# Lists of tokens: weights and columns of each list matmul laid side by side, made by thirds, multiplied in bursts of 16

## The chip, the cores and the metric

The kernel runs on one core of a Trainium2 chip. The metric is the device time of one execution in microseconds; the profile shows one execution. PE is TensorE, DVE VectorE, ACT ScalarE, POOL GpSimd, SP the queue that issues most DMAs. PEld is the loading of a matmul's weights. [...]

## The reference, cut to what matters

```python
N, D, E, F = 24576, 256, 8, 1024          # after FFT over (3072, 256) of 8 batches and a bilinear layer
logits = x @ w_gate                        # [N, E]
cap = N // E                               # 3072
for idx in np.argsort(-logits.flatten()):  # best pairs first
    tok, e = idx // E, idx % E
    if assigned[tok] >= 0 or counts[e] >= cap: continue
    assigned[tok] = e; counts[e] += 1
for e in range(E):
    mask = assigned == e
    out[mask] = np.maximum(x[mask] @ w1[e], 0.0) @ w2[e]
```

First come the Fourier transform of `x` along the sequence and the features (real part) and the layer `((x@w1) * (x@w2) @ w3) @ w_out`. Then each token goes to one of eight experts by the greedy rule above, each expert takes exactly 3072 tokens, and each expert is two matrices with a ReLU between.

## The kernel before, in words

Stage A (to about 1440 us) computes transform and layer and leaves 24576 rows in DRAM (`xs_d`) and the logits `L` in SBUF, as 128 partitions by 192 tiles (NT = 192) for each of the eight experts. The last part of its products is put off (`putoff`, L1338) and serves as TensorE's work while the first list is made.

Stage B works in eight phases (`ph`). For each phase `route` (L1121) finds which expert fills next, by two searches of eight counting rounds each for the 3072nd best logit, and then makes the **list** of the 3072 tokens of that expert, 24 of them in each of 128 partitions (CT = 24). The list is used as the index of gathers from DRAM (`gather`, L1407).

How the list is made: every token has a position 0 to 3071, or none. `rb` holds for each token (partition p, tile j) the row r (position modulo 128) and the column c (position divided by 128, plus 1). The list's entry (r, c) is the number of the token, 128 j + p. It is a sum over j of outer products: for each of the 192 tiles one matmul `li += oR[:, r | j]^T @ oC[:, c | j]` (L1281), with 128x128 bf16 weights that hold 1 where the token of partition p in tile j has row r, and 48 columns: 24 with p and 24 with j, where its column is c. `oR` and `oC` are made by comparisons on DVE: `X8` holds r minus a for a = 0..7, `C4` c minus a for a = 0..3 (L1256), and one instruction compares `X8` with 8r' to give eight rows at once (L1270), or `C4` with 4c'+1 for four columns (L1261). ACT makes the plane with p (L1262), DVE multiplies the other one by j (L1276). The tile number j is the innermost index, so the 128 weights of one matmul stand H elements apart (H = 60 in the first part) and its 48 columns 192 elements apart. `oR` is made in parts of 60, 60, 56 and 16 tiles (`PARTS`, L1039) in two buffers, and after each part its matmuls are issued in one block.

The order of work in stage B is written out by the program itself. The loop at L1583 goes over phases, six groups (`g`) of 512 tokens, and eight blocks (`f`) of 128 hidden units, here called steps. A step issues `first` (L1446: six matmuls of 512 columns into `hp`, L220 to L222), and `flush`/`second` (L1477: twelve of 256 columns into `yp`, L1487) for the step two before (LAG = 2). In f = 4 and 6 `turned` (L1429) transposes a block of the next group (L1432); DVE finishes it with L1440, and the split of the hidden values with L1470. ACT's share is L1436 and L1466.

Between these the routes run as generators: `lists()` (L1525) is called four times in a step and takes the next pieces of the route as long as the planner's clocks permit. The clocks are sums of estimated costs: `use("pe", 0.655)` for half of a `first` or `second`, a `yield` of so many us for DVE work, `use("a", ...)` for ACT. A `yield -2` holds the route until PE's planned clock has passed the others; a `yield -1` ends the call. When group 5 of a phase begins, the list of the next phase is demanded:

```python
if g == G - 1 and f == 0 and ph + 1 < E:
    while len(done) < ph + 2:
        next(gens[0])
    st = weights(which[ph + 1])
```

What is left of that list is then issued at once, whatever the clocks say. Each engine works through its own instructions in the order of issue. In the first route (L1557) there are no expert products yet, and each `yield` pays for steps of `putoff`, one per STEP = 0.26.

Of the kernel before, what the change touches and what calls it, by code (L numbers as in the profile page):

```python
# [9 lines left out]
F32 = mybir.dt.float32  # L10
F32R = mybir.dt.float32r
BF = mybir.dt.bfloat16
I32 = mybir.dt.int32
U32 = mybir.dt.uint32
U16 = mybir.dt.uint16
AF = mybir.ActivationFunctionType
ALU = mybir.AluOpType
# [5 lines left out]
NT = N // 128  # L23
CAP = N // E
CT = CAP // 128
# [995 lines left out]
def stage_b(ctx, tc, I, out, k):  # L1021
    nc, vec, act, pool = k.nc, k.vec, k.act, k.pool
    Lw = k.L
    cp_ = ctx.enter_context(tc.tile_pool(name="rconst", bufs=1))
# [6 lines left out]
    tri, trij, jrow, rank, ones = (rc[n].bitcast(BF) for n in ("tri", "trij", "jrow", "rank", "ones"))  # L1031
    pcol, rank9, id8, srch = (rc[n] for n in ("pcol", "rank9", "id8", "srch"))
# [3 lines left out]
    sg4, thr1, neg3 = srch[:, 64:68], srch[:, 68:71], srch[:, 71:74]  # L1036
    ident = k.sc["ident"]
    CHAIN = 0.45
    PARTS = (60, 60, 56, 16)  # L1039
    rt = ctx.enter_context(tc.tile_pool(name="rt", bufs=2))  # L1040
    ex = ctx.enter_context(tc.tile_pool(name="ex", bufs=2))
    blk = cp_.tile([128, 128], F32R, name="blk")
# [6 lines left out]
    vec.memset(zero, 0.0)  # L1049
    ecs = cp_.tile([128, 1], F32, name="ecs")  # L1050
    vec.memset(ecs, float(E * (E + 1) // 2))
    alive = cp_.tile([128, NT], F32, name="alive")
    vec.memset(alive, 1.0)

# [9 lines left out]
    clock = {"pe": 0.0, "v": 0.0, "a": 0.0, "d": 0.0}  # L1064

    def use(engine, cost, after=0.0):
        clock[engine] = max(clock[engine], after) + cost
        return clock[engine]


    def whole(b):
        return [128, b, NT]
# [18 lines left out]
    def small(shape, name, dt=F32):  # L1091
        return rt.tile([128] + shape, dt, name=name)
# [28 lines left out]
    def route(ph, done):  # L1121
# [3 lines left out]
        if ph < E - 1:  # L1125

            v = rt.tile([128, NT], F32, name="v", bufs=1)
            vec.tensor_reduce(v, Lw.rearrange("p e j -> p j e"), axis=AX.X, op=ALU.max)
            yield 1.7
            oh = rt.tile([128, E, NT], BF, name="X8", bufs=1)  # L1130
            vec.tensor_tensor(oh, Lw, v[:, None, :].to_broadcast(whole(E)), op=ALU.is_equal)
            yield 1.7
            vec.tensor_tensor(oh, oh, rank, op=ALU.mult)
            yield 0.9
            m4 = rt.tile([128, 4, NT], BF, name="C4", bufs=1)
            vec.tensor_tensor(m4, oh[:, 0:4], oh[:, 4:8], op=ALU.max)
            vec.tensor_tensor(m4[:, 0:2], m4[:, 0:2], m4[:, 2:4], op=ALU.max)
            code = rt.tile([128, NT], BF, name="code", bufs=1)
# [9 lines left out]
            hl = rt.tile([128, 2, NT], U16, name="hlv", bufs=1)  # L1148
            vec.tensor_tensor(hl, ky.bitcast(U16).rearrange("p (j h) -> p h j", h=2), alive[:, None, :].to_broadcast(whole(2)), op=ALU.mult)
            yield 0.9  # L1150
            planes = rt.tile([128, 2, CT, NT], BF, name="oC", bufs=1).rearrange("p a c j -> p (a c j)").bitcast(U16)
            quart = rt.tile([128, 128 * PARTS[0]], BF, name="oR", bufs=2).bitcast(U16)
            quart = [quart[:, i * E * NT:(i + 1) * E * NT] for i in range(4)]
            junk[:] = quart[2:]

# [83 lines left out]
        A = rt.tile([128, NT], F32, name="A", bufs=1)  # L1239
# [9 lines left out]
        rb = rt.tile([128, 2, NT], BF, name="rb", bufs=1)  # L1249
        vec.tensor_copy(rb, rc2)  # L1250
        yield 1.0
        X8 = rt.tile([128, 8, NT], BF, name="X8", bufs=1)
        C4 = rt.tile([128, 4, NT], BF, name="C4", bufs=1)
        for X, i, n in ((C4, 1, 4), (X8, 0, 8)):
            for a in range(n):
                vec.tensor_scalar(X[:, a], rb[:, i], float(a), None, op0=ALU.subtract)  # L1256
            yield 0.12 * n
        oC = rt.tile([128, 2, CT, NT], BF, name="oC", bufs=1)
        for c in range(CT // 4):
            c4 = slice(4 * c, 4 * c + 4)  # L1260
            vec.tensor_scalar(oC[:, 1, c4], C4, float(4 * c + 1), None, op0=ALU.is_equal)  # L1261
            act.activation(oC[:, 0, c4], oC[:, 1, c4], AF.Copy, scale=pcol)  # L1262
            use("a", 0.85, clock["v"])
            yield 0.3
        li = psum.tile([128, 512], F32, tag="rps", name="li", bufs=2)[:, :2 * CT]
        for h, H in enumerate(PARTS):
            j0 = sum(PARTS[:h])
            oR = rt.tile([128, 128 * PARTS[0]], BF, name="oR", bufs=2)[:, :128 * H].rearrange("p (r a j) -> p r a j", r=16, a=8)
            for r in range(16):
                vec.tensor_scalar(oR[:, r], X8[:, :, j0:j0 + H], float(8 * r), None, op0=ALU.is_equal)  # L1270
                if r % 4 == 3:
                    yield 0.27 + H / 110
            if h == 0:
                for c in range(3):
                    c8 = slice(8 * c, 8 * c + 8)
                    vec.tensor_tensor(oC[:, 1, c8], oC[:, 1, c8], jrow[:, None].to_broadcast(whole(8)), op=ALU.mult)  # L1276
                    yield 0.9
            yield -2
            use("pe", 0.027 * H)
            for jj in range(j0, j0 + H):  # L1280
                nc.tensor.matmul(li, oR[:, :, :, jj - j0].rearrange("p r a -> p (r a)"),  # L1281
                                 oC[:, :, :, jj].rearrange("p a c -> p (a c)"), start=jj == 0, stop=jj == NT - 1)
        yield -1
        ls = rt.tile([128, 2 * CT], F32, name="ls")
        vec.tensor_copy(ls, li)
# [3 lines left out]
        if ph < E - 1:  # L1289

            yield 0.2
            mem = rt.tile([128, NT], F32, name="mem", bufs=1)
            vec.tensor_scalar(mem, rb[:, 1], 0.5, None, op0=ALU.is_gt)
            vec.scalar_tensor_tensor(mem, rb[:, 1], CT + 0.5, mem, op0=ALU.is_lt, op1=ALU.mult)  # L1294
            vec.tensor_tensor(alive, alive, mem, op=ALU.subtract)
            yield 0.8
            el = small([E], "el")
            vec.tensor_scalar(el, rank9[:, :E], ec, -2.0, op0=ALU.is_equal, op1=ALU.mult)
            vec.tensor_scalar(el, el, 1.0, FMAX, op0=ALU.add, op1=ALU.mult)
            vec.tensor_tensor(Lw, Lw, el[:, :, None].to_broadcast(whole(E)), op=ALU.min)  # L1300
            yield 2.0
# [121 lines left out]
    def due():  # L1423
        todo = [e[1] for e in late if e[0] <= 0]
        late[:] = [[n - 1, fn] for n, fn in late if n > 0]
        for fn in todo:
            fn()
# [78 lines left out]
    FILL = 1.0, 1.0  # L1506
    PREP = 3
    DEEP = 7
    STEP = 0.26
# [4 lines left out]
    done, which, gens = [], [], []  # L1514
# [38 lines left out]

    with tc.manual_schedule(engines=ALL):
        head, wts, st, n = route(0, done), [], None, 0
        more, spare = putoff() if k.putoff else iter(()), 0.0
        while not done:  # L1557
            spare += FILL[bool(which)] * max(next(head), 0.0)
            while spare > 0 and more:
                spare -= STEP  # L1560
                if next(more, 0) == 0:
                    more = None
            if which and st is None:
                st = weights(which[0])
            n += st is not None
            if n > 13 and len(wts) < AHEAD:
                for _ in more or ():
                    pass
                more = None
                wts.append(chunk(st, len(wts)))  # L1570
        for _ in more or ():
            pass
        cur = group(0, 0, 0)
        clock.update(pe=10.0, v=0.0, a=0.0, d=0.0)
        due()
        while len(wts) < NF:
            wts.append(chunk(st, len(wts)))
        for kt in range(2):
            turned(cur["xg"], kt, cur["xh"], cur["xl"])
            due()  # L1580
            due()
        gens.append(x for gen in [head] + [route(ph, done) for ph in range(1, E)] for x in gen)
        for ph in range(E):  # L1583
            for g in range(G):
                for f in range(NF):
# [4 lines that stand above are left out]
                    if f == 0 and (ph, g) != (E - 1, G - 1):  # L1590
                        nxt = group(*((ph, g + 1) if g + 1 < G else (ph + 1, 0)))
                    lists()
                    pend.append((wts, f, first(wts, f, cur["xh"], cur["xl"], f % ONP[ph] == 1), cur))
                    due()
                    lists()
                    if len(pend) > LAG and (ph, g, f) != (E - 1, G - 1, NF - 1):
                        flush()
                    if f in (4, 6) and nxt:
                        turned(nxt["xg"], (f - 4) // 2, nxt["xh"], nxt["xl"])
                    due()  # L1600
                    if g == G - 1 and ph + 1 < E:
                        wnext.append(chunk(st, f))
                cur, nxt = nxt, None
            wts, wnext = wnext, []
        while late:
            due()

        grp = pend[0][3]
        yo = ex.tile([128, 4, D], F32, name="yo", bufs=PREP + 1)
        for i in range(4):  # L1610
            for w, f, hhl, _ in pend:
                second(w, f, hhl, grp["yp"], [i])
            act.activation(yo[:, i], grp["yp"][i], AF.Copy)
# [30 lines left out]
```

## Time and profile before

| | |
|---|---|
| runs | 2942.2 us median of three, 2933.6 to 2942.9 |
| profiled execution | 2939.1 us, span of the profile 2937.3 us |
| PE busy | 2799.5 us (95%) |
| PE weight loads busy | 2590.4 us (88%) |
| DVE busy | 2155.7 us (73%) |
| ACT busy | 1313.3 us (45%) |
| POOL busy | 1542.7 us (53%) |
| mean granted clock of PE | 0.961 |
| stage A, until about | 1440 us |
| first list | 1541 to 1559 us |
| lists 2 to 8 | between 1702 and 2658 us |

A matmul is pipelined: its time runs from its start to the arrival of its results, and the next one starts before. So distances between starts tell the rate, and a row that merges n matmuls gives it as (time of the row minus time of one) by n - 1. Busy time of PE is the union of such spans.

### The profile page before, as it was taken

What the parts mean: (1) busy time and instruction counts of PE and PEld (TensorE: products, weight loads), DVE (VectorE), ACT (ScalarE), POOL (GpSimd) and SP (SyncE); (2) the same over time, 40 slices, a digit from 0 to 9 for tenths busy, and PEclk for the clock granted to TensorE, in tenths of its full rate; (3) what the DMA queues carried; (4) which work ended last, traced back from release to release, by engine and by line L of the source; (5) the groups of instructions that cost most, each with busy time, mean ns of one, the idle gap of its engine ahead of it and who ended that gap; (6) DMA issues with size and microseconds to landing.
All of it is one profiled execution on the core that took longest, in us unless ns stands there. A gap on an engine that the chain in (4) does not pass through costs nothing.

```text
span 2937.3 us, 52341 instructions
## 1 busy us (share of the span) xinstructions
PE 2799.5 (95%) x19983; PEld 2590.4 (88%) x19983; DVE 2155.7 (73%) x4088; ACT 1313.3 (45%) x2350; POOL 1542.7 (53%) x1536
## 2 busy tenths in 40 slices
PE   4899999999999999999998899999999999999998
PEld 2799999999999999987897788989889898889997
DVE  9787787978878796888786878587786858752222
ACT  3343433434344343444363647374563736532332
POOL 7285775838577685944214253353534426343542
PEclk7999999999999999999997999999998989989999
DMA  5411110101011010155491121121112112111211
GB/s 199 139 59 38 37 45 23 63 19 52 30 37 52 25 57 16 50 186 202 163 357 46 33 69 44 58 55 66 48 44 62 52 51 60 40 55 41 71 46 37
DMA packets 104630, 207.63 MB, mean 71 GB/s; under 512 B 35162, under 2 KB 60426, under 8 KB 99002
## 3 DMA queue, kind: packets, MB, share of 16 engines
q1 hardware_dynamic: 81000, 131.02, 13.1%
q0 software_dynamic: 22144, 72.84, 7.7%
q8 instruction: 158, 2.59, 0.4%
q14 instruction: 94, 0.77, 0.1%
q10 hardware_dynamic: 1234, 0.41, 0.1%
HBM read 118.41 MB, written 80.28 MB: 68 GB/s over the span
## 4 chain that ended last, share of the span: by engine, by line
PE 65%; DVE 24%; ACT 4%; issue 3%; POOL 2%; DMA 1%; DVEq 0%; POOLq 0%; SPq 0%; ACTq 0%
PE yp L1487 11%; PE l L220 6%; PE l L222 6%; PE l L221 5%; PE li L1281 5%; DVE oR L1087 4%; PE hp L220 4%; PE hp L222 4%; PE hp L221 4%; PE acc L807 4%; PE acc L811 4%; PE acc L808 4%; DVE qs L866 3%; DVE pm L849 2%; PE l L843 2%
## 5 line engine op out<-in xcount | busy, mean ns | idle before, releaser
L861 POOL TENSOR_TENSOR al<-qs,ah 128x512 fp32r<-128x512 f32 x376 | 517.8, 1377 | 424.1 <-ACT ah L860 346.3
L1487 PE MATMUL yp<-FA,W 128*128 128x256 f32 x3040 | 629.8, 288 | 13.2 <-ACT yo L1493 5.6
L1487 PEld LDWEIGHTS yp<-FA,W 128*128 128x128 f32 x3040 | 504.6, 193 | 42.8 <-ACT yo L1493 15.6
L866 DVE TENSOR_TENSOR qs<-pm 128x512 f32<-128x512 f32 x384 | 398.9, 1039 | 36.3 <-DVE pm L850 1.4
L1470 DVE SCALAR_TENSOR_TENSOR W<-hp,W 128x512 fp32r<-128x512 f32 x336 | 229.5, 686 | 240.8 <-ACT W L1466 240.8
L849 DVE TENSOR_TENSOR pm<-l,qs 128x512 f32<-128x512 f32 x384 | 264.8, 690 | 172.5 <-PE l L222 146.7
L1487 PE MATMUL yp<-FB,W 128*128 128x256 f32 x1520 | 391.2, 283 | 0.0
L847 ACT ACTIVATE qs<-l 128x512 f32<-128x512 f32 x384 | 227.6, 593 | 332.1 <-PE l L222 315.4
L860 ACT ACTIVATE ah<-qs 128x512 fp32r<-128x512 f32 x376 | 236.8, 630 | 304.4 <-DVE qs L866 264.2
L1466 ACT ACTIVATE W<-hp 128x512 fp32r<-128x512 f32 x336 | 197.6, 595 | 353.0 <-PE hp L222 340.0
L220 PE MATMUL hp<-tabA,tabB 128*128 128x512 f32 x768 | 327.6, 427 | 1.3 <-ACT tabA L1436 1.3
L1497 POOL DMA_INDIRECT out_dram<-yo,oi x188 | 193.2, 1028 | 233.4 <-DMA out_dram<-yo,oi 215.0
L221 PE MATMUL hp<-tabA,tabB 128*128 128x512 f32 x768 | 310.0, 404 | 2.4 <-DVE tabA L1440 2.4
L1487 PEld LDWEIGHTS yp<-FB,W 128*128 128x128 f32 x1520 | 292.4, 192 | 16.6
L1411 POOL DMA_INDIRECT xt<-xs_d,idx x192 | 191.7, 999 | 210.5 <-DVE mem L1294 141.2
L807 PE MATMUL acc<-W,ah 128*128 128x264 f32 x1120 | 287.7, 287 | 15.0 <-DVE xo L919 14.9
L808 PE MATMUL acc<-W,ah 128*128 128x264 f32 x1120 | 285.9, 285 | 0.0
L1087 DVE TENSOR_SCALAR_CACHE_REDUCE oR<-oR,nx 128x1536 uint16<-128x1536 uint16 x196 | 282.0, 1459 | 0.0
L850 DVE TENSOR_TENSOR pm<-l,qs 128x512 f32<-128x512 f32 x384 | 261.1, 680 | 0.0
L222 PE MATMUL hp<-tabA,tabB 128*128 128x512 f32 x624 | 253.0, 406 | 0.0
L1461 POOL TENSOR_TENSOR W<-xo,W 128x512 fp32r<-128x512 f32 x48 | 79.4, 1654 | 319.0 <-ACT W L1459 318.8
L807 PEld LDWEIGHTS acc<-W,ah 128*128 128x128 f32 x1120 | 211.6, 189 | 17.8 <-DVE xo L919 17.7
(372 smaller groups left out, 7257.4 us busy)
## 6 DMA issues: line engine op xcount, KB each, us to landing
xs_d<-xo SPq DMA_DIRECT2D x96, 260.0 KB
xt<-in_xg_dram SPq DMA_DIRECT2D x24, 1024.0 KB
away<-ah SPq DMA_DIRECT2D x56, 256.0 KB
away<-al SPq DMA_DIRECT2D x56, 256.0 KB
yo<-away SPq DMA_DIRECT2D x28, 512.0 KB
raw<-in_w3t_dram SPq DMA_DIRECT2D x16, 512.0 KB
FA<-away SPq DMA_DIRECT2D x14, 512.0 KB
FB<-away SPq DMA_DIRECT2D x14, 512.0 KB
```

Of the source, the lines that this page charges most:

```text
L220: nc.tensor.matmul(out, ah, bh, start=start, stop=False, skip_group_check=True)
L221: nc.tensor.matmul(out, ah, bl, start=False, stop=False, skip_group_check=True)
L222: nc.tensor.matmul(out, al, bh, start=False, stop=stop, skip_group_check=True)
L807: nc.tensor.matmul(acc[i][:, :264], ah[:, a], W[0][:, f], start=f == 0, stop=False, skip_group_check=True)
L808: nc.tensor.matmul(acc[i][:, :264], ah[:, a], W[1][:, f], start=False, stop=False, skip_group_check=True)
L849: vec.tensor_tensor(pm[:, 0].rearrange("p w c -> p (w c)"), ue, qs, op=ALU.add)
L850: vec.tensor_tensor(pm[:, 1].rearrange("p w c -> p (w c)"), ue, qs, op=ALU.subtract)
L860: act.activation(ah, qs, AF.Copy)
L861: (vec if n == k.aside - 1 and f in LAST else pool).tensor_tensor(al, qs, ah, op=ALU.subtract)
L866: return ah, al, parts, lambda: vec.tensor_tensor(ab, pm[:, :, 0], pm[:, :, 1], op=ALU.mult)
L1087: vec.tensor_scalar(jk[:, :n], T[:, :n], nx[:, i:i + 1], None, op0=ALU.is_ge, op1=ALU.add, accum_out=acc[:, i:i + 1])
L1487: nc.tensor.matmul(yp[i], hhl[seq[s][0]][:, t[i]], seq[s][1], start=f == 0 and s == 0 and (i % 2 == 0 or len(yp) == 4), stop=f == NF - 1 a ...
```

## The change

`C4` becomes `C8` with eight columns, and both `X8` and `C8` are stored with the eight values of one tile side by side (tile outer, a inner). The list is made in three equal parts of 64 tiles. For each part `oC` is made as well as `oR`: three column comparisons of eight columns, one ACT copy, 16 row comparisons and one product with `j8` (the tile numbers, repeated eight times, made once). In `oR` the 128 weights of a tile are now neighbours; in `oC` the 48 columns of a tile are six runs of eight. `oC` has two buffers now. The 64 matmuls of a part are issued in bursts of 16 with a `yield -1` between, so that each burst takes a call of `lists()`. In the first route such a yield pays for one step of `putoff`. `mem` uses the tile of `A`.

```diff
-    PARTS = (60, 60, 56, 16)
+    PARTS, BURST = (64, 64, 64), 16
+    j8 = cp_.tile([128, NT, 8], BF, name="j8")
+    act.activation(j8, jrow[:, :, None].to_broadcast([128, NT, 8]), AF.Copy)
...
-            m4 = rt.tile([128, 4, NT], BF, name="C4", bufs=1)
+            m4 = rt.tile([128, 8, NT], BF, name="C8", bufs=1)[:, :4]
...
-            planes = rt.tile([128, 2, CT, NT], BF, name="oC", bufs=1).rearrange("p a c j -> p (a c j)").bitcast(U16)
-            quart = rt.tile([128, 128 * PARTS[0]], BF, name="oR", bufs=2).bitcast(U16)
+            planes = rt.tile([128, 2 * CT * PARTS[0]], BF, name="oC").bitcast(U16)
+            quart = rt.tile([128, 128 * PARTS[0]], BF, name="oR").bitcast(U16)
...
-        X8 = rt.tile([128, 8, NT], BF, name="X8", bufs=1)
-        C4 = rt.tile([128, 4, NT], BF, name="C4", bufs=1)
-        for X, i, n in ((C4, 1, 4), (X8, 0, 8)):
-            for a in range(n):
-                vec.tensor_scalar(X[:, a], rb[:, i], float(a), None, op0=ALU.subtract)
-            yield 0.12 * n
-        oC = rt.tile([128, 2, CT, NT], BF, name="oC", bufs=1)
-        for c in range(CT // 4):
-            c4 = slice(4 * c, 4 * c + 4)
-            vec.tensor_scalar(oC[:, 1, c4], C4, float(4 * c + 1), None, op0=ALU.is_equal)
-            act.activation(oC[:, 0, c4], oC[:, 1, c4], AF.Copy, scale=pcol)
-            use("a", 0.85, clock["v"])
-            yield 0.3
+        X8, C8 = (rt.tile([128, 8, NT], BF, name=n, bufs=1).rearrange("p a j -> p (a j)").rearrange("p (j a) -> p j a", a=8)
+                  for n in ("X8", "C8"))
+        for X, i in ((C8, 1), (X8, 0)):
+            for a in range(8):
+                vec.tensor_scalar(X[:, :, a], rb[:, i], float(a), None, op0=ALU.subtract)
+            yield 1.2
...
-            oR = rt.tile([128, 128 * PARTS[0]], BF, name="oR", bufs=2)[:, :128 * H].rearrange("p (r a j) -> p r a j", r=16, a=8)
+            js = slice(j0, j0 + H)
+            oC = rt.tile([128, 2 * CT * PARTS[0]], BF, name="oC")[:, :2 * CT * H].rearrange("p (n c j a) -> p n c j a", n=2, c=CT // 8, a=8)
+            oR = rt.tile([128, 128 * PARTS[0]], BF, name="oR")[:, :128 * H].rearrange("p (j r a) -> p r j a", r=16, a=8)
+            for c in range(CT // 8):
+                vec.tensor_scalar(oC[:, 1, c], C8[:, js], float(8 * c + 1), None, op0=ALU.is_equal)
+            act.activation(oC[:, 0], oC[:, 1], AF.Copy, scale=pcol)
+            use("a", 1.7, clock["v"] + 0.6)
+            yield 0.6
             for r in range(16):
-                vec.tensor_scalar(oR[:, r], X8[:, :, j0:j0 + H], float(8 * r), None, op0=ALU.is_equal)
+                vec.tensor_scalar(oR[:, r], X8[:, js], float(8 * r), None, op0=ALU.is_equal)
                 if r % 4 == 3:
-                    yield 0.27 + H / 110
-            if h == 0:
-                for c in range(3):
-                    c8 = slice(8 * c, 8 * c + 8)
-                    vec.tensor_tensor(oC[:, 1, c8], oC[:, 1, c8], jrow[:, None].to_broadcast(whole(8)), op=ALU.mult)
-                    yield 0.9
+                    yield 0.85
+            vec.tensor_tensor(oC[:, 1], oC[:, 1], j8[:, None, js].to_broadcast([128, CT // 8, H, 8]), op=ALU.mult)
+            yield 0.95
             yield -2
-            use("pe", 0.027 * H)
-            for jj in range(j0, j0 + H):
-                nc.tensor.matmul(li, oR[:, :, :, jj - j0].rearrange("p r a -> p (r a)"),
-                                 oC[:, :, :, jj].rearrange("p a c -> p (a c)"), start=jj == 0, stop=jj == NT - 1)
+            for jj in range(H):
+                if jj % BURST == 0:
+                    if jj:
+                        yield -1
+                    use("pe", 0.02 * BURST)
+                nc.tensor.matmul(li, oR[:, :, jj].rearrange("p r a -> p (r a)"), oC[:, :, :, jj].rearrange("p n c a -> p (n c) a"), start=j0 + jj == 0, stop=j0 + jj == NT - 1)
...
-            mem = rt.tile([128, NT], F32, name="mem", bufs=1)
+            mem = rt.tile([128, NT], F32, name="A", bufs=1)
...
-            spare += FILL[bool(which)] * max(next(head), 0.0)
+            v = next(head)
+            spare += FILL[bool(which)] * max(v, 0.0) + (v == -1) * STEP
```

## Rows read from the trace of the kernel before

**Rows 1.** One window; busy us (x count) of PE, PEld, DVE, ACT, POOL; PEclk; DMA.
```profile
1700.00:2670.00 970.00, 953.38 (x6486) 862.64 (x6485) 707.43 (x1815) 500.23 (x888) 428.33 (x434) 0.94 0.18 54
```

**Rows 2.** Timeline of PE around list 2: start us, us, what, count.
```profile
1700.21 0.40 PE L220 MATMUL hp<-tabA,tabB 128*128 128x512 f32 x1
...
1701.60 0.28 PE L1487 MATMUL yp<-FA,W 128*128 128x256 f32 x1
...
1702.31 5.50 PE L1281 MATMUL li<-oC,oR 128*128 128x48 bf16 x60
1707.60 0.37 PE L1487 MATMUL yp<-FA,W 128*128 128x256 f32 x1
...
1709.36 0.77 PE L220 MATMUL hp<-tabA,tabB 128*128 128x512 f32 x1
...
1710.79 5.53 PE L1281 MATMUL li<-oC,oR 128*128 128x48 bf16 x60
1716.10 0.77 PE L220 MATMUL hp<-tabA,tabB 128*128 128x512 f32 x1
...
1725.82 0.78 PE L220 MATMUL hp<-tabA,tabB 128*128 128x512 f32 x1
...
1728.53 0.29 PE L1487 MATMUL yp<-FA,W 128*128 128x256 f32 x1
```

**Rows 3.** Windows around the first list and list 2, columns as in rows 1.
```profile
1542.00:1559.00 17.00, 16.60 (x186) 16.37 (x184) 9.60 (x49) 3.14 (x11) 2.02 (x3) 0.50 0.03 10
...
1700.00:1740.00 40.00, 40.00 (x317) 37.13 (x316) 25.72 (x71) 8.22 (x18) 15.14 (x14) 0.87 0.22 73
```

**Rows 4.** Line L1281, all lists: duration ns min/median/max, first and last start.
```profile
L1281 PEld LDWEIGHTS <-oR x1536: 140/145/178, 1541.2 to 2657.1; 128*128 128x128 bf16 x192
L1281 PE MATMUL li<-oC,oR x1536: 260/267/307, 1541.2 to 2657.2; 128*128 128x48 bf16 x192
```

**Rows 5.** Line L1229 (ranks), and one of its places on PE's timeline.
```profile
L1229 PEld LDWEIGHTS <-M x24: 96/98/100, 1528.4 to 2604.8; 128*128 128x128 bf16 x24
L1229 PE MATMUL rps<-xt,M x24: 219/219/230, 1528.4 to 2604.9; 128*128 128x128 bf16 x24
...
1528.37 0.34 PE L1229 MATMUL rps<-xt,M 128*128 128x128 bf16 x3
```

**Rows 6.** Timeline around the first list: row comparisons on DVE, matmuls on PE.
```profile
1534.95 3.18 DVE L1270 TENSOR_SCALAR oR<-X 128x480 bf16<-128x480 bf16 x16
...
1541.09 5.39 DVE L1270 TENSOR_SCALAR oR<-X 128x480 bf16<-128x480 bf16 x16
...
1541.23 17.37 PE L1281 MATMUL li<-oC,oR 128*128 128x48 bf16 x192 [3.72 <-DVE oC L1276]
```

**Rows 7.** Timeline of PE at one counting round of a search.
```profile
1459.41 0.17 PE L1102 MATMUL rps<-cnt,blk 128*128 128x4 f32 x1
1459.43 0.25 PE L1103 MATMUL rps<-cnt,half 128*128 128x4 f32 x1
```

**Rows 8.** Timeline of DVE and PE around list 4's first block.
```profile
2023.49 1.09 DVE L1256 TENSOR_SCALAR X<-rb 128x192 bf16<-128x192 bf16 x8
...
2027.11 0.88 DVE L1261 TENSOR_SCALAR oC<-C 128x768 bf16<-128x768 bf16 x3
...
2032.99 2.69 DVE L1276 TENSOR_TENSOR oC<-oC,xt 128x1536 bf16<-128x1536 bf16 x3
...
2037.47 1.78 PE L1281 MATMUL li<-oC,oR 128*128 128x48 bf16 x18
...
2047.46 0.48 PE L220 MATMUL hp<-tabA,tabB 128*128 128x512 f32 x1
...
2048.38 0.69 DVE L1440 TENSOR_TENSOR tabA<-tp,tabA 128x512 fp32r<-128x512 f32 x1 [1.31 <-ACT tabA L1436]
```

**Rows 9.** DVE by form (count, busy us, mean ns), and L1159 (ns min/median/max).
```profile
L1128 DVE TENSOR_REDUCE v<-L 128x192 f32<-128x1536 f32 x7 | 20.8, 2971 | 0.1
...
L1159 DVE TENSOR_TENSOR oC<-X,hlv x14: 945/950/2142, 1446.8 to 2440.1; 128x1536 uint16<-128x1536 bf16 x14
```

## The prediction

> **What bounds the kernel now.** I read the page first: TensorE (PE) is busy 95% of the span (table above). A share over all stages can hide another limit, so the second view is a window. From 1700 to 2670 us, where seven of the eight lists are made beside the expert products, PE is busy 953 of 970 us and VectorE (DVE) 707 [rows 1]. The reader is to see that here whatever leaves PE's queue comes off the time, as long as nothing new keeps PE waiting, and that DVE has slack, but not much. The granted clock is 0.94.
>
> The third view is PE's order around one list [rows 2]. A step of the expert loop is six hp matmuls (1.39 us) and twelve yp (1.42, six in 0.71), 2.8 us together. The list comes in blocks, here 60 matmuls in 5.50 us and 60 in 5.53, each 0.27 us from its start to its end, so 59 distances take 5.23 us: **89 ns each**. After a block ordinary matmuls run slow for a while: six hp from 1725.82 need 2.71 us and not 1.39. [...]
>
> The fourth view is one matmul. List matmuls have 48 columns and take 267 ns, with weight loads of 145 ns [rows 4]. The bf16 matmuls that build the ranks have 128 columns and contiguous weights, and take 219 ns with loads of 98 [rows 5]. Fewer columns, yet longer. A column is worth 0.43 ns (hp with 512 columns 0.39 us, yp with 256 0.28 [rows 2]), so 48 should end after 185 ns; the 82 ns too many are 1.7 on each column, and the load's 47 too many fall on its weights. What the two have in common is layout: weights 120 bytes apart, columns 384 bytes apart. Columns at 0.43 + 1.7 ns would take 102 ns each matmul, the 89 lie between. The first list went at 90 ns as well (192 in 17.37 us [rows 6]) though its clock was 0.50 [rows 3], so the array's clock isn't what sets it.
>
> **The change part by part.**
>
> *List matmuls.* Weights become 128 neighbours, columns six runs of eight. Upper bound for the new spacing: bf16 pairs with 128 columns, three in 0.34 us, the last ending 0.22 after its start, so 60 ns [rows 5]. Lower bound: two matmuls of 4 columns in the threshold search start 20 ns apart at this view's rounding [rows 7]. 60 ns less the 80 columns that a list matmul has fewer (34 ns) is 26, near the low end; but three instructions are no stream, and 64 in a row must load 64 weights, so I take 35 ns. Saved: 192 x 54 = 10.4 us a list, **72.6 us** for seven; bounds 192 x 29 x 7 = 39 and 192 x 62 x 7 = 83.
>
> *Clock.* In the list of [rows 2] six yp and four transposes from 1707.60 on lost about 0.6 of their 1.76 us, three hp from 1709.36 0.74, three from 1716.10 as much, six from 1725.82 1.3. Together 3.4 us, of 10.4 us at the low level (0.13 x 2 x 40). The whole window has 0.06 x 2 x 970 = 116 us at the low level, so some 40 us are lost. Bursts of 16 short matmuls between stretches of 0.7 us of ordinary ones give the array more to do than 5 us of 89-ns matmuls, but a wait and a block of 64 remain (below). I take half back: **20 us**; bounds 0 and 40.
>
> *DVE for the first third.* Before, behind X8: 6 column compares of 0.29 us, 16 row compares in 3.2, 3 products in 2.7 [rows 6, 8]: 7.6 us. After: 3 compares of 512 elements (0.2 each), 16 row compares of 512 (3.4, scaled from 480), one product (0.9): 4.9. The row compares now write runs of 16 bytes, 256 bytes apart, which no row shows. Nearest is the product into planes with runs of 32 bytes, 950 ns for 1536 elements as in the contiguous product of the list (2.7 for three) [rows 8, 9], so I charge nothing; the other bound is rival 1. X8 and C8 become 16 instructions that write single elements 16 bytes apart, where 12 took 0.13 us each [rows 8]. Not in the trace either. Lower bound 0.13; upper from the reduction that reads elements 768 bytes apart: 2971 ns for 1536, 1.93 each [rows 9], so 0.37 + 0.06 = 0.43. I take 0.25, 4.0 us for 1.55. The chain to the first block comes out 0.2 us shorter (bounds 2.2 shorter, 2.6 longer). [...]
>
> The planner counts on less: its yields before the first block add up to 0.7+1.0+0.48+0.96+1.8+3.26+2.7 = 10.9 before and 0.7+1.0+2.4+0.6+3.4+0.95 = 9.05 after, so PE comes 2.0 us of real time earlier (a step that it counts as 2.62 takes 2.80). DVE's slack is 1.8 us now (products done at 2035.68, first list matmul at 2037.47 [rows 8]). Wait 0.4 us a list with rounding, **3 us** in all; bounds 0 and 20.
>
> *Where the blocks fall.* I went through lists() and the loop around it with the planner's own numbers (yield and use), for order alone. For the kernel before that puts the parts of 60, 60, 56, 16 into steps 4 to 7 of group 4, and the list is done at the first step of group 5, just where the next phase demands it. With the new yields each third takes four calls of lists(), a block of 16 in each. In lists 3 to 7 the first two thirds fit; of the last, 12 of 16 row compares, the product and all 64 matmuls are left when group 5 demands the list, and go out in one piece: PE stands until DVE has finished. DVE can begin that third when it has done the transposed block of step 6 (L1440): where one is seen beside PE, it ends at 2049.07 and the next step began at 2047.46 [rows 8], so about 1.6 us into step 7. PE then has 1.2 us of step 7 and three bursts (1.7 us) left, DVE 4.9: wait 2.0, with the handover 2.3 us. Five times that, 1 us for list 2 (there it is three bursts and a whole third), 0.5 for list 8, which nothing demands early: **13 us**; bounds 5 and 28. Queued behind the waiting matmuls are all expert products, and ScalarE and DVE wait for those.
>
> *Switching.* The first yp after a block takes 0.37 us, others 0.28 [rows 2]. Five more changes a list: **4 us**.
>
> *First list.* It stands on the path: 17.4 us of PE alone [rows 6]. After, DVE sets the pace: first third at about 1541, then two of 4.9 to 6.5 us (16 row compares took 5.39 us while GpSimd worked, 3.18 without [rows 6]), then 64 matmuls of 40 ns at the low clock: 1553 to 1557 for 1558.6. **4 us** gained; bounds 1 and 6.
>
> *Hidden.* ScalarE's one copy of 1536 for two of 768 lies under the row compares (3.4 us; half of it would show if they were gone); j8 is made once beside the postponed products; mem in A's place and second oC buffers only meet readers that are done; the extra postponed step per burst finds nothing left, since 1.2+1.2+0.6+3.4 us of yields come before the first burst.
>
> Sum: 72.6 + 20 - 3 - 13 - 4 + 4 = 76.6 us. The profiled execution took 2939.1 us (span 2937.3), so **2863 us**. The runs' median of 2942.2 is 3 us above it, within their spread of 9; that spread, 0.3%, is also about what this kernel's measurement tells from no change.
>
> **Rivals.**
>
> 1. *Slower: DVE's short runs.* If a row compare with 16-byte runs costs more than the 0.2 us at which they follow each other now, each 0.1 us puts 1.6 us on every third, and PE waits for all three: 4.8 us a list, 34 in seven. The gain is gone at 0.42 us each. At the 1.93 ns per element of the spread reads [rows 9], 1.05 us each, it would be 3150 us, and a third of the way there 2960. For it: nothing in the trace writes so. Against: 32-byte runs at full rate.
>
> 2. *The pair doesn't get below what a short bf16 stream shows.* At 60 ns the saving is 39 us, the clock returns perhaps 10, the waits stay: 39 + 10 - 16 - 4 + 3 = 32, so 2907 us. For it: the row itself, if loads set it. Against: 4-column matmuls 20 ns apart. [...]
>
> 3. *The spacing stays at 89 ns.* Then layout was not its cause; bursts, waits and clock are left: 0 to 20 back, 20 lost, 2939 to 2960. Against it stand both durations of [rows 4, 5].
>
> 4. *Better: no waits, the whole clock, 28 ns.* 82 + 40 - 4 + 5 = 123 less: 2816.
>
> **How the numbers follow.** Forecast 0.70 (its own range 2835 to 2900), rival 4 0.06, rival 2 0.10, rival 1 0.09 (half of it past the break-even), rival 3 0.05. Leaving out the slow cases and the best gives 2825 to 2915. Faster 0.87 (forecast, 4, 2, a part of 1), same 0.05, slower 0.08.
>
> **What would show it.** List matmuls near 185 ns, loads near 98, a burst of 16 in 0.7 us; a granted clock above 0.96 from 1700 on; PE idle 2 to 3 us before the last 64, ended by DVE's product. I would be wrong if row compares of 512 follow each other at 0.4 us or more, if loads stay at 145 ns, or if the clock still falls three times a list.

## The result, and the profile after

The changed kernel takes **2861.5 us** (median of four runs, 2860.15 to 2862.58), the kernel before 2941.4 beside it. The ratio is 0.9733, interval 0.9715 to 0.9751. Forecast were 2863 us, with 2825 to 2915 as the range. The profiled execution took 2861.26 us with a span of 2859.5; that is 77.8 us of span less than before. One execution of the kernel in experiment 2 ran in a slower state (3651.88 us at a mean granted clock of 0.679) and is left out of the figures below.

The page's busy shares and its row of granted clock (PEclk, in tenths of the full clock), over 40 slices of the span:

```profile
PE 2681.1 (94%) x19983; PEld 2469.2 (86%) x19983; DVE 2194.8 (77%) x4016; ACT 1310.1 (46%) x2327; POOL 1568.5 (55%) x1536
...
PEclk7999999999999999999998999999999999999999
```

Next, windows of the changed kernel: the first list, the stretch of lists 2 to 8 (it answers to [rows 1]), and 40 us each around lists 3 and 5 (columns as in [rows 1]; PEclk is the granted clock as a share of the full one).

```profile
1543.00:1555.00 12.00, 8.04 (x192) 7.90 (x192) 9.29 (x40) 6.83 (x14) 11.94 (x4) 0.50 0.04 14
...
1697.00:2588.00 891.00, 842.89 (x6472) 748.42 (x6471) 742.27 (x1750) 500.88 (x873) 444.59 (x434) 0.99 0.20 58
...
1845.00:1885.00 40.00, 37.20 (x385) 32.77 (x384) 31.52 (x87) 15.84 (x26) 15.74 (x15) 0.96 0.23 78
...
2172.00:2212.00 40.00, 37.22 (x395) 32.88 (x394) 32.00 (x85) 17.62 (x30) 17.59 (x16) 1.00 0.23 81
```

Three things have moved against [rows 1]. The clock of the stretch is 0.99 instead of 0.94; around a list it is 0.96 or 1.00, where it was 0.87 [rows 3]. PE is now idle for 48 of 891 us; before it was 17 of 970. DVE is busy 83% of the stretch instead of 73%. TensorE has become faster, and part of what it won is now lost in waiting for DVE.

The line of the list matmuls, all eight lists (min/median/max in ns), answers to [rows 4]:

```profile
L1284 PEld LDWEIGHTS <-oR x1536: 95/96/119, 1542.9 to 2587.9; 128*128 128x128 bf16 x192
L1284 PE MATMUL li<-oC,oR x1536: 182/183/220, 1542.9 to 2588.0; 128*128 128x48 bf16 x192
```

PE's timeline shows the first list, list 3, list 5's last block and a place in list 8 (start, us, what, count, idle time before and what ended it):

```profile
1542.92 2.74 PE L1284 MATMUL li<-oC,oR 128*128 128x48 bf16 x64 [6.19 <-DVE oC L1276]
1547.63 2.72 PE L1284 MATMUL li<-oC,oR 128*128 128x48 bf16 x64 [1.97 <-DVE oC L1276]
1552.34 2.72 PE L1284 MATMUL li<-oC,oR 128*128 128x48 bf16 x64 [1.99 <-DVE oC L1276]
...
1855.86 0.57 PE L1284 MATMUL li<-oC,oR 128*128 128x48 bf16 x16
...
1873.64 2.29 PE L1284 MATMUL li<-oC,oR 128*128 128x48 bf16 x64 [1.82 <-DVE oC L1276]
...
1876.33 0.63 PE L221 MATMUL hp<-tabA,tabB 128*128 128x512 f32 x1
...
2199.34 1.76 PE L1284 MATMUL li<-oC,oR 128*128 128x48 bf16 x64 [1.82 <-DVE oC L1276]
...
2547.57 1.22 PE L1489 MATMUL yp<-FA,W 128*128 128x256 f32 x4 [5.42 <-DVE W L1472]
```

A block of 64 takes 1.76 us, at a granted clock of 1.00 (list 5's last), so 63 distances take 1.76 - 0.18 = 1.58: **25 ns** each, where it was 89. In the first list, at a clock of 0.50, it is (2.72 - 0.18) / 63 = 40 ns. Lists 3 to 7 come in eight bursts of 16 and then 64 in one piece, and before these 64 PE stands for 1.8 us, ended by DVE's product: this is the demanded last third of the prediction. In list 3 the clock is low for a moment in and behind this block: 0.64 from 1873.64 to 1876.30 us and 0.50 from there to 1877.00 (block 2.29 us, hp 0.63). The wait of 5.42 us in list 8 was not foreseen. It is for the hidden split of an expert (W, L1472), and DVE's timeline says why:

```profile
2001.78 3.67 DVE L1259 TENSOR_SCALAR C<-rb 128x192 bf16<-128x192 bf16 x8
2005.89 0.68 DVE L1442 TENSOR_TENSOR tabA<-tp,tabA 128x512 fp32r<-128x512 f32 x1
2006.48 3.84 DVE L1259 TENSOR_SCALAR X<-rb 128x192 bf16<-128x192 bf16 x8
...
2032.51 3.31 DVE L1273 TENSOR_SCALAR oR<-X 128x512 bf16<-128x512 bf16 x16
2035.74 0.95 DVE L1276 TENSOR_TENSOR oC<-oC,j 128x1536 bf16<-128x1536 bf16 x1
...
2534.89 5.67 DVE L1259 TENSOR_SCALAR C<-rb 128x192 bf16<-128x192 bf16 x8
2540.17 5.42 DVE L1259 TENSOR_SCALAR X<-rb 128x192 bf16<-128x192 bf16 x8
...
2546.84 0.68 DVE L1472 SCALAR_TENSOR_TENSOR W<-hp,W 128x512 fp32r<-128x512 f32 x1
```

The 16 row compares and the product cost what they did before (0.2 us apart, and 0.95). The 16 writes to X8 and C8 do not: in list 4 they follow each other at 0.43 us (0.41 on average, as the first follows sooner), against 0.13 in [rows 8]. In list 8 four of the distances are 0.9 to 2.1 us and the others as in list 4, so that the writes hold DVE for 10.7 us on end, with the split queued behind them. The writes with these distances stand beside GpSimd's work. The longest of all writes to X8 (first row, min/median/max in ns) starts at 2540.60, takes 2.44 us and spans two tensor_tensors of GpSimd:

```profile
L1259 DVE TENSOR_SCALAR X<-rb x64: 587/836/2442, 1534.4 to 2544.8; 128x192 bf16<-128x192 bf16 x64
...
2541.16 0.74 POOL L1405 TENSOR_TENSOR tabB<-ste,tabB 128x256 fp32r<-128x256 f32 x1
2541.86 0.73 POOL L1405 TENSOR_TENSOR FB<-ste,FA 128x256 fp32r<-128x256 f32 x1
```

GpSimd's timeline beside list 4's writes shows one more thing: the gather that began with them took 3.71 us instead of 1.00 and ended as the first eight ended (2005.57 and 2005.45).

```profile
2000.55 1.00 POOL L1413 DMA_INDIRECT xt<-xs_d,idx  x1 [0.30 <-issue]
2001.86 3.71 POOL L1413 DMA_INDIRECT xt<-xs_d,idx  x1 [0.30 <-issue]
```

The view of waits over the stretch (us in total, times, longest) has 17.4 us of PE waiting for the split, and 5.8 us for the transposed block that DVE finishes between the two sets of eight writes (tabA, L1442). The last row is the split's in the kernel before.

```profile
PE yp L1489 <- DVE W L1472: 17.4, 15, 5.4
PE li L1284 <- DVE oC L1276: 12.7, 11, 2.0
PE hp L221 <- DVE tabA L1442: 5.8, 5, 1.2
...
PE yp L1487 <- DVE W L1470: 2.9, 9, 0.5
```

### The profile page after: what moved, and what is told of

Read it like the earlier page. It is cut to its first block, busy times and chain, and to the rows that moved or that the text cites. A ratio compares the mean times of both kernels' runs of the same rounds, so it can differ in the third digit from the quotient of the medians.

```text
span 2859.5 us, 52239 instructions
## 1 busy us (share of the span) xinstructions
PE 2681.1 (94%) x19983; PEld 2469.2 (86%) x19983; DVE 2194.8 (77%) x4016; ACT 1310.1 (46%) x2327; POOL 1568.5 (55%) x1536
## 4 chain that ended last, share of the span: by engine, by line
PE 61%; DVE 29%; issue 4%; ACT 4%; POOL 1%; DMA 1%; DVEq 0%; ACTq 0%; SPq 0%; POOLq 0%
PE yp L1489 11%; PE l L220 6%; PE l L222 6%; PE l L221 6%; DVE oR L1089 4%; PE acc L807 4%; PE acc L811 4%; PE acc L808 4%; PE hp L220 4%; DVE qs L866 3%; PE hp L222 3%; PE hp L221 3%; DVE pm L849 2%; DVE W L1472 2%; PE l L843 2%
## 5 line engine op out<-in xcount | busy, mean ns | idle before, releaser
L1489 PE MATMUL yp<-FA,W 128*128 128x256 f32 x3040 | 620.0, 285 | 30.0 <-DVE W L1472 20.8
L1489 PEld LDWEIGHTS yp<-FA,W 128*128 128x128 f32 x3040 | 494.5, 189 | 60.5 <-DVE W L1472 24.5
L1472 DVE SCALAR_TENSOR_TENSOR W<-hp,W 128x512 fp32r<-128x512 f32 x336 | 231.2, 691 | 207.0 <-ACT W L1468 207.0
L1499 POOL DMA_INDIRECT out_dram<-yo,oi x188 | 200.6, 1067 | 234.4 <-DMA out_dram<-yo,oi 212.7
L220 PE MATMUL hp<-tabA,tabB 128*128 128x512 f32 x768 | 321.9, 419 | 0.0
L221 PE MATMUL hp<-tabA,tabB 128*128 128x512 f32 x768 | 303.5, 395 | 7.6 <-DVE tabA L1442 7.6
L1413 POOL DMA_INDIRECT xt<-xs_d,idx x192 | 209.8, 1093 | 112.4 <-DVE A L1296 51.4
L222 PE MATMUL hp<-tabA,tabB 128*128 128x512 f32 x624 | 247.2, 396 | 0.0
L1463 POOL TENSOR_TENSOR W<-xo,W 128x512 fp32r<-128x512 f32 x48 | 71.2, 1483 | 309.9 <-ACT W L1461 309.6
```

What stands on the lines that cost most here:

```text
L220: nc.tensor.matmul(out, ah, bh, start=start, stop=False, skip_group_check=True)
L221: nc.tensor.matmul(out, ah, bl, start=False, stop=False, skip_group_check=True)
L222: nc.tensor.matmul(out, al, bh, start=False, stop=stop, skip_group_check=True)
L1472: vec.scalar_tensor_tensor(hl, hp, 0.0, hh, op0=ALU.max, op1=ALU.subtract)
L1489: nc.tensor.matmul(yp[i], hhl[seq[s][0]][:, t[i]], seq[s][1], start=f == 0 and s == 0 and (i % 2 == 0 or len(yp) == 4), stop=f == NF - 1 a ...
```

## The experiments

The theory: the layout alone sets the 25 ns, each operand with its own limit; bursts and thirds by themselves give nothing; the 16 writes are the cost that was sized wrong. The rivals: short bursts keep the granted clock up and bring part of the gain; or columns and weights share one limit.

**1. The old layout, with the new thirds and bursts.**

```diff
-        X8, C8 = (rt.tile([128, 8, NT], BF, name=n, bufs=1).rearrange("p a j -> p (a j)").rearrange("p (j a) -> p j a", a=8)
-                  for n in ("X8", "C8"))
+        X8, C8 = (rt.tile([128, 8, NT], BF, name=n, bufs=1) for n in ("X8", "C8"))
...
-            oC = rt.tile([128, 2 * CT * PARTS[0]], BF, name="oC")[:, :2 * CT * H].rearrange("p (n c j a) -> p n c j a", n=2, c=CT // 8, a=8)
-            oR = rt.tile([128, 128 * PARTS[0]], BF, name="oR")[:, :128 * H].rearrange("p (j r a) -> p r j a", r=16, a=8)
+            oC = rt.tile([128, 2 * CT * PARTS[0]], BF, name="oC")[:, :2 * CT * H].rearrange("p (n c a j) -> p n c a j", n=2, c=CT // 8, a=8)
+            oR = rt.tile([128, 128 * PARTS[0]], BF, name="oR")[:, :128 * H].rearrange("p (r a j) -> p r a j", r=16, a=8)
```

> Thirds, bursts of 16 and second oC buffers as in the changed kernel, but tile number innermost again in X8, C8, oR and oC (weights 128 bytes apart, columns 128 bytes apart). Theory (layout sets the spacing of list matmuls): 89 ns again, so 192 x 64 ns x 7 = 86 us come back, less some 10 us because X8 and C8 are written side by side: about 2940 us, no faster than the kernel before. The granted clock should fall less than before, since bursts are short. Rival (short bursts and equal thirds give the gain, through the clock and a smoother order): at most 2890 us.

Measured: 2987.25 us (2983.64 to 2987.88), ratio 1.0145 [1.0128, 1.0162]. That is slower than the kernel before, and by more than expected. The line of the list matmuls, and a block of 64 on PE's timeline:

```profile
L1284 PEld LDWEIGHTS <-oR x1536: 161/182/244, 1539.4 to 2712.2; 128*128 128x128 bf16 x192
L1284 PE MATMUL li<-oC,oR x1536: 260/312/378, 1539.4 to 2712.4; 128*128 128x48 bf16 x192
...
2267.77 7.84 PE L1284 MATMUL li<-oC,oR 128*128 128x48 bf16 x64
```

(7.84 - 0.31) / 63 = 120 ns in this block (126 is the median distance in all of the run's lists) and not 89. These matmuls differ from those of [rows 4] in distances alone: thirds of 64 put the weights 128 bytes apart, where parts of 60 put them 120, and the columns 128, where they were 384. Spacing is a matter of layout, then, but the expectation of 89 took the old layout for the same at any distance. The mean clock of this kernel is 0.953 (0.961 before), although its bursts are of 16.

**2. The old layout at its old distance.** As in 1, but with weights and columns 120 bytes apart (parts of 60, 60, 60, 12), so that, beside thirds and bursts, only the columns' distance (384 bytes before) differs from the kernel before.

```diff
-    PARTS, BURST = (64, 64, 64), 16
+    PARTS, BURST = (60, 60, 60, 12), 16
...
+            oR = rt.tile([128, 128 * 60], BF, name="oR").rearrange("p (r a j) -> p r a j", r=16, a=8)[:, :, :, :H]
```

> Weights and columns both 120 bytes apart, X8 and C8 as before, with the changed kernel's parts-by-parts order and bursts of 16 (parts of 60, 60, 60 and 12). Theory (the 126 ns of the first old-layout run came from the 128-byte distance; layout sets the spacing, bursts give little): 85 to 92 ns, and 2930 to 2950 us, the kernel before give or take 10. Rival (short bursts help even so): 2900 to 2920 us.

Measured: 2934.91 us (2927.41 to 2944.82), ratio 0.9983 [0.9969, 0.9997]; the time is in the range expected, the spacing a little above it.

```profile
L1284 PEld LDWEIGHTS <-oR x1536: 143/148/177, 1534.2 to 2672.0; 128*128 128x128 bf16 x192
L1284 PE MATMUL li<-oC,oR x1536: 251/278/313, 1534.2 to 2672.1; 128*128 128x48 bf16 x192
...
2234.99 7.11 PE L1284 MATMUL li<-oC,oR 128*128 128x48 bf16 x72
```

(7.11 - 0.28) / 71 = 96 ns, loads as in [rows 4]. Without the layout the change is worth 0.2%. As pairs at 96 and not 89 ns cost 192 x 7 ns x 7 = 9 us, thirds and bursts by themselves are worth more than that, some 14 us (an estimate), but not 80. The run also shows the distance: in the same layout 96 ns with both operands at 120 bytes, 120 with both at 128.

**3. Columns side by side, weights (and X8) as before.** Weights 128 bytes apart in one kernel; 120 in the other, by parts of 60, 60, 60 and 12:

```diff
-            oR = rt.tile([128, 128 * PARTS[0]], BF, name="oR")[:, :128 * H].rearrange("p (j r a) -> p r j a", r=16, a=8)
+            oR = rt.tile([128, 128 * PARTS[0]], BF, name="oR")[:, :128 * H].rearrange("p (r a j) -> p r a j", r=16, a=8)
...
+            oR = rt.tile([128, 128 * 60], BF, name="oR").rearrange("p (r a j) -> p r a j", r=16, a=8)[:, :, :, :H]
```

> New layout for oC and C8 alone; oR and X8 with the tile number innermost (weights 128 bytes apart). Theory (columns set the 89 ns, weights come next): matmuls near 183 ns, loads near 145 ns, spacing 50 to 65 ns, so 192 x 7 x 32 ns = 43 us more than the changed kernel, less some 5 us for X8: 2890 to 2905 us. Rival (weights set it): spacing 85 to 89 ns and about 2940 us.

> As the run with the new column layout alone, but with weights 120 bytes apart, as in the kernel before, not 128; parts of 60, 60, 60 and 12. Theory (at 128 bytes the weights are slow for a reason of their own; at 120 the columns set the 89 ns before): loads 145 ns, matmuls 183 ns, spacing 50 to 70 ns, and 2890 to 2910 us. Rival (weights anywhere apart are enough to hold the pair near 89 ns): spacing 85 to 89 ns and 2930 to 2945 us.

Measured: at 128 bytes 2932.27 us (2923.93 to 2933.33), 0.9961 [0.9947, 0.9975]; at 120 bytes 2891.74 (2891.19 to 2894.89), 0.9838 [0.9823, 0.9853]. First the rows of the kernel at 128 bytes, then those of the one at 120:

```profile
L1284 PEld LDWEIGHTS <-oR x1536: 164/212/252, 1541.0 to 2650.5; 128*128 128x128 bf16 x192
L1284 PE MATMUL li<-oC,oR x1536: 185/249/293, 1541.0 to 2650.6; 128*128 128x48 bf16 x192
...
2232.51 5.84 PE L1284 MATMUL li<-oC,oR 128*128 128x48 bf16 x64
```

```profile
L1284 PEld LDWEIGHTS <-oR x1536: 141/168/181, 1540.4 to 2628.5; 128*128 128x128 bf16 x192
L1284 PE MATMUL li<-oC,oR x1536: 182/221/250, 1540.4 to 2628.6; 128*128 128x48 bf16 x192
...
2213.52 4.69 PE L1284 MATMUL li<-oC,oR 128*128 128x48 bf16 x72
```

(5.84 - 0.25) / 63 = 89 ns at 128 bytes, (4.69 - 0.22) / 71 = 63 at 120. The first missed its expectation of 50 to 65 and 2890 to 2905 us and came out nearer to its rival; by itself it read as if columns were worth next to nothing. The second, with the weights at the distance that the kernel before had, falls into its ranges: against experiment 2 the columns' layout alone takes 96 to 63 ns.

**4. Weights side by side, tile number innermost in the columns** (they are 128 bytes apart, 384 in the kernel before):

```diff
-            oC = rt.tile([128, 2 * CT * PARTS[0]], BF, name="oC")[:, :2 * CT * H].rearrange("p (n c j a) -> p n c j a", n=2, c=CT // 8, a=8)
+            oC = rt.tile([128, 2 * CT * PARTS[0]], BF, name="oC")[:, :2 * CT * H].rearrange("p (n c a j) -> p n c a j", n=2, c=CT // 8, a=8)
```

> New layout for oR and X8 alone; oC and C8 with the tile number innermost (columns 128 bytes apart). Theory (columns set the 89 ns): loads near 96 ns, matmuls near 265 ns, spacing still 85 to 89 ns: about 2940 us. Rival (weights set it): spacing near 25 ns and 2855 to 2865 us.

Measured: 2914.22 us (2911.88 to 2918.86), 0.9905 [0.9888, 0.9923]: a spacing just below what was expected (85 to 89 ns), a time some 26 us better. Most of that should be the clock, 0.98 from 1700 to 2600 us for 0.94 before (an estimate: at 0.94 the products lost 39 us at the low level).

```profile
L1285 PEld LDWEIGHTS <-oR x1536: 95/116/147, 1542.2 to 2638.5; 128*128 128x128 bf16 x192
L1285 PE MATMUL li<-oC,oR x1536: 241/262/287, 1542.2 to 2638.6; 128*128 128x48 bf16 x192
...
2226.68 5.58 PE L1285 MATMUL li<-oC,oR 128*128 128x48 bf16 x64
```

(5.58 - 0.26) / 63 = 84 ns. So 48 columns 128 bytes apart hold a pair at 84 ns, 128 weights apart at 63 (120 bytes) or 89 (128); both apart hold it at 89 (120 and 384 bytes, the kernel before), 96 or 120. Either alone is enough to keep a pair far from 25. Columns alone at 384 bytes were not run. With both operands apart the granted clock doesn't set the spacing: the first list of the kernel before, at 0.50, went at 90 ns [rows 3, 6], and its block of [rows 2] at 1702.31, at 1.00, at 89, while pairs with both operands side by side go from 25 ns at 1.00 to 40 at 0.50. For the 84 ns here that was not shown.

**5. Blocks of 64 instead of bursts of 16.**

```diff
-    PARTS, BURST = (64, 64, 64), 16
+    PARTS, BURST = (64, 64, 64), 64
```

> The changed kernel with one block of 64 per third. Theory: spacing stays at 25 ns, a block lasts 1.6 us; the planner gets through the list in fewer calls, so nearly nothing of the last third is left when the list is demanded, and the wait of 2 us before the last block shrinks: 2850 to 2862 us. [...]

Measured: 2843.44 us (2839.31 to 2845.83), 0.9656 [0.9638, 0.9674]; 18 us less than the changed kernel, and better than the 2850 to 2862 expected. The three blocks of list 3 on PE's timeline, and the stretch of lists:

```profile
1854.96 1.76 PE L1284 MATMUL li<-oC,oR 128*128 128x48 bf16 x64 [0.34 <-DVE oC L1276]
1864.28 1.78 PE L1284 MATMUL li<-oC,oR 128*128 128x48 bf16 x64
1872.73 1.78 PE L1284 MATMUL li<-oC,oR 128*128 128x48 bf16 x64
```

```profile
1700.00:2567.00 867.00, 831.92 (x6447) 741.60 (x6446) 735.57 (x1750) 498.66 (x870) 454.68 (x431) 0.99 0.20 59
```

But for 0.3 us before the first block of lists 3 to 7, no block of these lists waits for its third: the matmuls of a third go out in one call of the planner's and not in four, so the demand of the next phase finds nothing left. The wait before the last 64 is gone (but for list 2, 1.64 us), and so are the slow hp matmuls behind it (0.63 us at 1876.33 in the changed kernel) and six changes a list. The clock is 0.99 with these blocks as with the bursts: with pairs at 25 ns the rival, that the bursts keep the clock up, falls. With slow pairs it holds in part. The same stretch in experiments 2 and 1:

```profile
1700.00:2685.00 985.00, 963.96 (x6564) 870.70 (x6564) 715.27 (x1876) 509.37 (x889) 427.55 (x442) 0.96 0.18 54
...
1700.00:2725.00 1025.00, 1008.74 (x6559) 914.35 (x6558) 710.52 (x1753) 508.11 (x880) 425.62 (x438) 0.92 0.18 51
```

Experiment 2 has slower pairs than the kernel before, 96 ns for 89, and yet a clock of 0.96 where that had 0.94; so thirds and bursts keep some of the clock there. By the distances of their starts the matmuls of the experts' products lose 25 us at the low level in its lists 2 to 8 where they lost 39 before; that is the size of its 14 us. (The kernel of experiment 3 with weights at 128 bytes has 89 ns and 0.97.) At 120 ns a clock of 0.92 is left in spite of the bursts.

**6. X8 and C8 by two operations instead of 16.**

```diff
-            for a in range(8):
-                vec.tensor_scalar(X[:, :, a], rb[:, i], float(a), None, op0=ALU.subtract)
+            vec.tensor_tensor(X, rb[:, i, :, None].to_broadcast([128, NT, 8]), a8[:, None, :].to_broadcast([128, NT, 8]), op=ALU.subtract)
```

(a8 holds 0 to 7, set once.)

> The changed kernel with X8 and C8 made by one subtraction of two operands each (all eight values of a tile from one read of rb and a constant 0 to 7) in place of 16 instructions that write single elements 16 bytes apart. Theory (those 16 cost DVE 7 us a list and make PE wait, 0.5 us twice before the first third, 5.6 us once before the last list): two of about 1.7 us, 4 us less DVE a list, and 2848 to 2856 us. Rival (covered, PE waits elsewhere): within 3 us of the changed kernel, 2858 to 2864.

Measured: 2840.74 us (2837.04 to 2845.1), 0.9656 [0.9643, 0.9669]; 21 us less than the changed kernel, where 5 to 13 were expected. The line that makes the marks (min/median/max):

```profile
L1261 DVE TENSOR_TENSOR C<-rb,a x8: 1758/1759/1760, 1537.0 to 2521.5; 128x1536 bf16<-128x1536 bf16 x8
L1261 DVE TENSOR_TENSOR X<-rb,a x8: 1751/1797/2855, 1538.7 to 2523.2; 128x1536 bf16<-128x1536 bf16 x8
```

3.6 us a list instead of 7 to 11, and at most 2.9 for one of the two. The stretch of lists, and PE's wait for the split in it:

```profile
1698.00:2572.00 874.00, 839.55 (x6471) 749.73 (x6470) 722.82 (x1666) 501.00 (x873) 432.80 (x434) 0.99 0.21 60
```

```profile
PE yp L1491 <- DVE W L1474: 12.3, 11, 2.0
```

PE is idle for 34 us of the stretch instead of 48. Its waits for the split fall from 17.4 to 12.3; those for the transposed block (5.8) and before the first 16 matmuls of lists 3 to 7 (0.3 each) are gone. What is left for the split stands mostly behind the demanded thirds and isn't due to the writes: two waits of 1.1 and 1.3 us behind list 3's in the changed kernel, 0.8 and 1.3 here. The profiled executions differ by 16 us, the medians by 21. So 16 writes in place of two operations cost 16 to 21 us; 3 were forecast for the whole term.

**7. Both.** Experiments 5 and 6 together.

> One block of 64 per third, and X8 and C8 by two subtractions. If both gains add: 2843 less 5 to 13, so 2830 to 2838 us, the fastest of all. If the blocks' gain was the same wait that the two subtractions remove: 2841 to 2845.

Measured: **2820.94 us** (2818.34 to 2827.25), 0.9600 [0.9585, 0.9615], the fastest, 1.4% below the changed kernel and below the 2830 to 2838 expected. The gains add: 18 + 21 = 39 of 41. The stretch of lists, and PE's wait for the split in it:

```profile
1691.00:2540.00 849.00, 825.31 (x6442) 739.98 (x6441) 716.49 (x1664) 500.31 (x870) 440.78 (x432) 1.00 0.21 61
```

```profile
PE yp L1491 <- DVE W L1474: 5.0, 14, 0.5
```

PE is idle for 24 of 849 us, and the longest wait for the split is 0.5 us; the longest of all is one of 5.9 us for the transposed block (hp, L221) before list 8.

## Why the prediction was right

The time came out 1.5 us from the forecast, and the mechanism is the one named: layout. But the sum hid terms that were off, in opposite directions.

- **List matmuls: too small.** 35 ns were taken, 25 measured, a little under the low bound. 192 x 64 ns x 7 = 86 us instead of 72.6. The loads and durations forecast (98 and 185 ns) came out at 96 and 183. The caution "three instructions are no stream" cost 13 us: a stream of 64 with loads goes nearly at the 20 ns that two 4-column matmuls showed. Rival 2 falls: the 60 ns of three pairs with 128 columns [rows 5] are no floor for 48, which go at 25.
- **Which operand.** Forecast was that columns 384 bytes apart explain the 89 ns and weights the longer loads. Experiments 3 and 4 bear it out as far as they go: with weights at the old 120 bytes, columns put right leave 63 ns; weights put right leave 84, with columns at 128 bytes and not 384.
- **Clock: too small.** The forecast takes the low level for half the full clock. The trace of the kernel before has it so: over the six hp of [rows 2] that take 2.71 us (1725.80 to 1728.60) the granted clock was 0.51, over the six that take 1.39 (1700.20 to 1701.60) it was 1.00. By the distances of their starts, the matmuls of the experts' products lost 39 us at the low level in lists 2 to 8 before (hp 0.43 us apart instead of 0.23, yp 0.21 instead of 0.12) and 7 after: 32 back for 20, within the bounds of 0 and 40. The reason given is only half right, since blocks of 64 keep the clock as well as bursts when pairs are fast (experiment 5), and bursts of slower pairs keep it in part or not at all (experiments 2 and 1). That a denser stream is the cause is argued, not shown by itself.
- **Last third: right.** Waits of 1.8 us before the last 64 in lists 3 to 7, 1.99 in list 2: 11 us for 13.
- **DVE for the first third: the term that was mis-sized.** "I take 0.25" for a write of single elements 16 bytes apart: it was 0.43, the upper bound (whose 0.06 us for each instruction was the author's estimate, which no row shows), where the contiguous writes of [rows 8] took 0.13. The step that failed is that the wait was looked for only at the first block of the list. There it came to 0.3 us in lists 3 to 7, for 0.4 forecast. But the writes keep all that is queued behind them on DVE: the transposed block, with 1.0 to 1.2 us of PE's time before each of these lists, and the hidden split, 5.4 us in list 8. PE's idle time in the stretch rose by 31 us; without the 11 of the last third that is 20 where 3 were forecast, at the term's upper bound. 14 of them go with the writes (experiment 6), most of the rest are waits for the split behind the demanded thirds, which no term held.
- **Row compares of 16-byte runs: right.** 16 in 3.31 us, 0.2 apart. Rival 1 falls.
- **First list: about right.** DVE sets its pace, as forecast, with PE waiting 1.97 and 1.99 us for its thirds. The 40 ns at the low clock, for which no row stood, came out at 40 at a granted clock of 0.50. The list ends at 1552.34 + 2.72 = 1555.06, where the one of [rows 6] ended at 1558.60; as the first list begins at 1541.2 us in the kernel before, at 1542.9 in the changed one and between 1534.2 and 1547.5 in the experiments, 4 us can't be told from 3.5.

The stretch with measured terms: 86 + 32 = 118 us less work for PE, of which its busy time shows 953 - 843 = 110; the 8 between them are what the more frequent changes between list and products can have cost (forecast 4, not measured by itself). Less the 31 us of idle time that leaves 79, from 970 to 891, and the span fell by 77.8. The list term and the clock were 25 us too small in the forecast, DVE's waits and the changes 21. A forecast that hits with errors of this size is luck in its number, worth less than its distance says.

Open is why 128 bytes between neighbours are slower than 120; the runs measure it and no more. That four single writes of list 8 take 1.3 to 2.4 us, where the others take 0.6 to 0.9, because GpSimd works beside them is what the trace suggests: those that do stand beside its tensor_tensors, and in the kernel before five contiguous writes of list 8 took 0.75 to 0.78 us instead of 0.2, beside such ones too. So the spread layout isn't needed for it; it wasn't tried alone.

## What to carry to other kernels

When a matmul with fewer columns takes longer than its neighbours, look at how its two operands lie in memory, and put both side by side: with the new thirds and bursts, columns alone gave 49 of 80 us here with weights 120 bytes apart, but 11 with weights 128 apart; weights alone gave 29. Then price what builds the new layout in instructions that write single elements far apart, and follow not only who reads the result but who is queued behind on the engine. Whether work should come in many small pieces is a question of its own; here three large ones left the planner nothing to demand.

## What was not expected of the hardware

- Pairs of weight load and matmul (bf16, 128x128 weights, 48 columns) with both operands side by side run 25 ns apart in a stream of 64 at a granted clock of 1.00, and 40 ns apart at 0.50.
- Pairs whose operands lie 128 bytes apart are slower than at 120: 89 against 63 ns with spread weights alone, 120 against 96 with both.
- Writes of 192 single bf16 elements, 16 bytes apart, follow each other at 0.43 us, and one tensor_tensor writes the same 1536 in order in 1.76.
- A GpSimd gather that began with such a run of writes took 3.71 us instead of 1.00.
